# One broadcast load instead of four, VectorE work metered by time, and two small moves, in a kernel of two attention blocks

## The chip, the cores and the metric

One Trainium2 chip, one core. The time is the device time of one execution in microseconds (us). Most executions of a kernel agree within about half a percent here; every ratio below is between runs of the state "fast" made on the same chip in the same rounds; where ratios of different rounds are set side by side, the text says so. A run counts as slow when it is over 1.5% above the fastest of its kernel. Ratios of times are the mean time of one kernel's fast runs over the mean time of the other's fast runs of the same rounds, so they are not quite the ratio of the medians quoted beside them, which take in the slow runs too.

## The reference

Two independent attention blocks over 2048 tokens, width 448, 16 heads of 28 columns; their outputs stand side by side.

```python
# A: plain multi-head attention
p = softmax(q @ k.T * Dh ** -0.5);  a = (p @ v) @ wo
# B: four segments of 512 tokens; inside a segment causal attention,
#    and from the second segment on a memory of the segments before
a_dot = softmax(q @ k.T * Dh ** -0.5 + mask) @ v
num, den = phi(q) @ M, phi(q) @ z + 1e-06          # phi(t) = t+1 if t>0 else exp(t)
o = g * (num / den) + (1 - g) * a_dot              # g = sigmoid(beta), one per head
M = M + phi(k).T @ v;  z = z + sum(phi(k))
b = concat(o) @ wo
```

## The kernel before

The kernel is a static program of 375 slots. In each slot PE makes the scores of three banks (3 x 512 columns), ScalarE takes the exponential of all three in one instruction, and PE multiplies an earlier result by V. Everything else (projections, transposes, output products) is put between, a piece a slot. In PSUM the program holds six banks for scores, and a ring of two banks for all the rest, which VectorE evicts (copies out of PSUM, so that the bank is free again). VectorE also computes 60 banks of exponentials of its own in six instructions each: the eviction and five deferred ones.

Sixteen heads are handled four at a time; heads sit at partitions 0, 32, 64, 96. A finished accumulator holds the unnormalised output and, in row 28 of each head, the sum of the weights. To divide, the program turns the sums into reciprocals and spreads them over the 32 partitions of their head. That goes through DRAM in hops. "Planes" is 1 for A and for the first segment of B, 2 where a memory product is normalised as well:

```python
    def finish(key):                       # an accumulator is complete
        planes = 2 if side == "B" and s >= 1 else 1
        nc.vector.tensor_copy(out=o[:], in_=a[:])
        for n in range(planes):            # 4 rows of sums to DRAM
            nc.sync.dma_start(out=d1[n], in_=os_[n][DH:P:HP, :])
        def hop1():                        # 2 slots later: back, spread over 128 partitions
            nc.sync.dma_start(out=r[:, 0:planes, :], in_=d1...)
            later(3, step2)
        def step2():
            if planes == 2:
                nc.vector.tensor_scalar_add(r[:, 1, :], r[:, 1, :], 1e-6)
            nc.vector.reciprocal(r[:, 0:planes, :], r[:, 0:planes, :])
            ...                            # B: one multiply by a coefficient per plane
            nc.sync.dma_start(out=d2[0:planes]..., in_=r[:, 0:planes, :])
            at(state["u"] + 3, hop2)
        def hop2():                        # one row of 512 floats to 32 partitions, four times a plane
            for n in range(planes):
                bc = nrm.tile([P, CW], FP32, tag="nrm", name="bc")
                for j in range(4):
                    src = d2[n, j, :]
                    nc.sync.dma_start(out=bc[j * HP:(j + 1) * HP, :],
                        in_=bass.AP(tensor=src.tensor, offset=src.offset,
                                    ap=[[0, HP], [1, CW]]))
            later(4, *[lambda n=n: mul(n) for n in range(planes)])   # VectorE: o * bc
            if planes == 2:
                later(4, add)
```

`later(d, ...)` puts VectorE work into a queue, due d slots on. At the end of a slot's VectorE work this rule takes from it:

```python
    def run_bg(limit):                     # limit is 2
        for n in range(limit):
            ready = [x for x in bg if x[0] <= state["u"]]
            if not ready or n and len(ready) < 3 and limit < 8:
                return
            ...                            # run the oldest
```

The softmax here doesn't subtract the row's maximum and nothing guards it: scores larger than these inputs give would overflow.

## Time and profile before

| | before |
|---|---|
| median time, first 6 runs / all 20 runs beside the changed kernel | 559.06 / 559.37 us |
| span of the profiled run | 558.0 us |
| exponentials of ScalarE | 375, 1.33 us from start to start when nothing holds them |
| excess of ScalarE over 1.33 us each, sum | 30.2 us |
| of it at 0-40 / 40-160 / 160-200 / 200-380 / 380-end us | 5.2 / 2.4 / 1.7 / 10.8 / 10.1 us |

The excess is worked out from the trace: the start-to-start distance of neighbouring exponentials less 1.33 us, summed. Its parts leave out intervals with another ScalarE instruction between.

From the page of the kernel before: busy time of the engines, the granted PE clock in 40 slices of the span (tenths), the shares of the chain that ended last, and the costliest group (line, engine, operation, tiles, shapes, count | busy us, mean ns | idle before it, and who ended that).

```profile
PE 511.9 (92%) x5646; PEld 214.2 (38%) x5646; DVE 398.2 (71%) x919; ACT 526.2 (94%) x401; POOL 67.0 (12%) x136
PEclk9999999999999999999999999999999999978999
PE 39%; ACT 27%; DVE 19%; issue 10%; DMA 3%; SPq 2%; POOL 0%; DVEq 0%; ACTq 0%
L378 ACT ACTIVATE pt<-ps_s 128x1536 bf16<-128x1536 f32 x375 | 512.5, 1505 | 19.0 <-PE ps_s L373 17.5
```

ScalarE (ACT) is busy 94% of the span and bounds the kernel; its idle time ends when PE delivers scores. The clock dips once, in slices 36 and 37.

The waits list of the kernel before (engine, line, waited for: us in total, times, longest us), cut to ScalarE and to VectorE's waits for transfers:

```profile
ACT pt L378 <- PE ps_s L373: 17.5, 34, 1.9
...
DVE r L508 <- DMA r<-d_8398: 1.8, 1, 1.8
...
DVE oT L535 <- DMA bc<-d_6268: 1.0, 1, 1.0
```

VectorE (DVE) waited 1.0 us for a broadcast in the whole run. What the clock dip came from is read from three timelines of the kernel before (start us, us, what; in brackets the idle time before and who ended it). First SP, the queue that issues the loads:

```profile
488.10 1.03 SPq L495 DMA_DIRECT2D d_8398<-osb  x2
489.23 3.97 SPq L525 DMA_DIRECT2D bc<-d_8240  x8
493.24 0.42 SPq L500 DMA_DIRECT2D r<-d_8398  x1
```

Then VectorE:

```profile
493.17 0.39 DVE L596 CAST y<-ps_y 128x224 bf16<-128x224 f32 x1 [0.36 <-PE ps_y L590]
495.35 0.17 DVE L508 TENSOR_SCALAR r<-r 128x16 f32<-128x16 f32 x1 [1.79 <-DMA r<-d_8398]
495.56 0.35 DVE L509 RECIPROCAL r<-r 128x32 f32<-128x32 f32 x1
495.95 0.37 DVE L512 TENSOR_SCALAR r<-r,coef 128x16 f32<-128x16 f32 x2
496.23 0.38 DVE L596 CAST y<-ps_y 128x224 bf16<-128x224 f32 x1
```

Then PE:

```profile
494.53 0.40 PE L454 MATMUL acc<-pt,vA 128*32 128x512 bf16 x4
496.67 0.91 PE L590 MATMUL ps_y<-woA,oT 128*128 128x224 bf16 x4 [1.74 <-DVE y L596]
497.51 0.61 PE L373 MATMUL ps_s<-qTA,kTA 32*128 32x512 bf16 x3
```

Eight issues for one two-plane finish held SP for 4 us. The load of `r` stood behind them, VectorE stood before `r` for 1.79 us with an eviction behind it, PE idled 1.74 us for that eviction, and three score products then took 0.61 us instead of about 0.39: the trace records half the clock from 496.5 us for 10.24 us.

The other kind of stall is a queue in front of VectorE. VectorE at 357 us, kernel before:

```profile
357.23 0.69 DVE L489 COPY osb<-acc 128x512 f32<-128x512 f32 x1 [0.15 <-PE acc L454]
357.83 0.50 DVE L338 TENSOR_SCALAR vz<-vy 128x512 f16<-128x512 uint16 x1
358.37 0.43 DVE L343 TENSOR_TENSOR vq<-vz 128x512 f16<-128x512 f16 x1
358.83 0.29 DVE L344 TENSOR_SCALAR vz<-vz 128x512 f16<-128x512 f16 x1
359.04 0.69 DVE L476 COPY osb<-ps_mem 128x512 f32<-128x512 f32 x1
```

Two evictions (L489, L476) have deferred work between them; PE idled 1.02 us until the second, ScalarE 0.96 us.

### The profile page before, as it was taken

Reading aid. Unit: us, or ns where it says so; the run is one execution under the profiler, and the core shown is the slowest. Engines: PE = TensorE matmul, PEld = TensorE weight load, DVE = VectorE, ACT = ScalarE, POOL = GpSimd, SP = SyncE. Lnnn points to the kernel's source line nnn. Section 1 sums busy time; section 2 is a strip of 40 time slices with the busy share of each in tenths; the row PEclk is TensorE's granted clock in tenths of the full one; section 3 lists DMA queues with packets and bytes.
Section 4 is the critical chain, followed back from the end, with each engine's and each line's share of the span. In section 5 each row is a group of like instructions: output and inputs, shape, how many; then the busy total and the mean of one; then the engine's idle time right before and its main releaser. Section 6 shows DMA issues by size and latency. Waiting matters only on the chain.

```text
span 558.0 us, 13768 instructions
## 1 busy us (share of the span) xinstructions
PE 511.9 (92%) x5646; PEld 214.2 (38%) x5646; DVE 398.2 (71%) x919; ACT 526.2 (94%) x401; POOL 67.0 (12%) x136
## 2 busy tenths in 40 slices
PE   8899999999999998999989988889999998989996
PEld 4443443434443434334334333333344343323332
DVE  3438877776867587667687788875887886968742
ACT  5799999999999999999999999899999999978994
POOL 9100000000000000040040220210400401600000
PEclk9999999999999999999999999999999999978999
DMA  9100021000030110002002002012031031134121
GB/s 251 27 1 3 22 57 32 19 5 23 2 108 1 55 35 22 2 4 71 12 6 79 3 26 59 2 26 75 3 96 59 6 93 35 33 92 112 35 61 51
DMA packets 33623, 23.78 MB, mean 43 GB/s; under 512 B 16780, under 2 KB 27660, under 8 KB 33560
## 3 DMA queue, kind: packets, MB, share of 16 engines
q1 hardware_dynamic: 32216, 21.89, 14.0%
q0 software_dynamic: 416, 0.81, 0.7%
q8 instruction: 44, 0.72, 0.5%
q10 hardware_dynamic: 928, 0.21, 0.2%
q14 instruction: 19, 0.16, 0.1%
HBM read 18.51 MB, written 4.37 MB: 41 GB/s over the span
## 4 chain that ended last, share of the span: by engine, by line
PE 39%; ACT 27%; DVE 19%; issue 10%; DMA 3%; SPq 2%; POOL 0%; DVEq 0%; ACTq 0%
ACT pt L378 26%; PE ps_s L373 8%; PE acc L454 8%; PE ps_s L360 6%; PE ps_proj L209 5%; PE ps_v L223 5%; DVE osb L489 3%; SPq L525 2%; DVE vq L343 2%; DVE vy L334 1%; DVE vz L338 1%; DVE ve L351 1%; DVE vz L344 1%; PE ps_y L590 1%; DMA wstB<-in_B_wv_dram 1%
## 5 line engine op out<-in xcount | busy, mean ns | idle before, releaser
L378 ACT ACTIVATE pt<-ps_s 128x1536 bf16<-128x1536 f32 x375 | 512.5, 1505 | 19.0 <-PE ps_s L373 17.5
L373 PE MATMUL ps_s<-qTA,kTA 32*128 32x512 bf16 x964 | 129.3, 388 | 4.8 <-ACT pt L378 2.6
L454 PE MATMUL acc<-pt,vA 128*32 128x512 bf16 x964 | 124.3, 393 | 0.0
L360 PE MATMUL ps_s<-warm 128*128 128x512 bf16 x292 | 93.2, 382 | 11.8 <-ACT pt L378 10.1
L394 POOL TENSOR_SCALAR_AFFINE_SELECT pt<-pt 128x256 bf16<-128x256 bf16 (+5 forms) x110 | 52.1, 497 | 420.8 <-ACT pt L378 420.7
L373 PEld LDWEIGHTS <-kTA 32*128 32x128 bf16 x964 | 34.3, 91 | 94.2 <-issue 90.5
L454 PEld LDWEIGHTS <-vA 128*32 128x32 bf16 x1024 | 31.2, 93 | 71.6 <-issue 71.6
L209 PE MATMUL ps_proj<-xT,wstB 112*32 112x256 bf16 x1024 | 42.8, 274 | 7.8 <-DVE kTB L216 2.2
L209 PE MATMUL ps_proj<-xT,wstA 112*32 112x256 bf16 (+3 forms) x960 | 41.3, 281 | 1.5 <-DVE vy L334 0.5
L351 DVE SCALAR_TENSOR_TENSOR ve<-vy,vq 128x512 int16<-128x512 int32 x60 | 42.1, 702 | 0.3
L360 PEld LDWEIGHTS <-warm 128*128 128x128 bf16 x292 | 24.4, 97 | 39.8 <-issue 36.5
L223 PEld LDWEIGHTS <-xT 112*128 112x128 bf16 x352 | 28.2, 97 | 21.1 <-issue 19.0
L209 PEld LDWEIGHTS <-wstB 112*32 112x32 bf16 x1024 | 28.9, 96 | 18.4 <-issue 14.7
L209 PEld LDWEIGHTS <-wstA 112*32 112x32 bf16 x960 | 26.6, 95 | 14.2 <-issue 12.4
L596 DVE CAST y<-ps_y 128x224 bf16<-128x224 f32 x48 | 18.7, 389 | 18.0 <-PE ps_y L590 17.5
L489 DVE COPY osb<-acc 128x512 f32<-128x512 f32 x31 | 21.4, 690 | 9.4 <-PE acc L454 8.3
L343 DVE TENSOR_TENSOR vq<-vz 128x512 f16<-128x512 f16 x60 | 26.9, 448 | 1.6
L348 DVE TENSOR_TENSOR vq<-vq,vz 128x512 f16<-128x512 f16 x60 | 27.0, 451 | 0.2
L338 DVE TENSOR_SCALAR vz<-vy 128x512 f16<-128x512 uint16 x60 | 25.9, 431 | 1.1
L454 PE MATMUL acc<-ve,vA 128*32 128x512 bf16 x60 | 23.9, 399 | 0.0
L216 DVE TENSOR_SCALAR kTA<-ps_proj,live 128x256 bf16<-128x256 f32 (+3 forms) x29 | 14.8, 511 | 11.6 <-PE ps_proj L209 10.8
L454 PE MATMUL acc<-pt,vB 128*32 128x512 bf16 (+3 forms) x256 | 23.0, 306 | 0.0
(233 smaller groups left out, 491.7 us busy)
## 6 DMA issues: line engine op xcount, KB each, us to landing
out_dram<-y SPq DMA_DIRECT2D x32, 112.0 KB
xn<-in_A_x_dram SPq DMA_DIRECT2D x4, 448.0 KB
xnB<-in_B_x_dram SPq DMA_DIRECT2D x4, 448.0 KB
wstA<-in_A_wqkv_dram SPq DMA_DIRECT2D x2, 290.5 KB
bc<-d_4323 SPq DMA_DIRECT2D x8, 64.0 KB
bc<-d_4985 SPq DMA_DIRECT2D x8, 64.0 KB
bc<-d_5650 SPq DMA_DIRECT2D x8, 64.0 KB
bc<-d_6337 SPq DMA_DIRECT2D x8, 64.0 KB
```

The lines of the kernel that those rows point to most:

```text
L209: nc.tensor.matmul(ps[j * HP:(j + 1) * HP, a:b], lhsT=w[:, c, h0:h0 + HP], rhs=xT[:, c, sc * CW + a:sc * CW + b], start=(c == 0), stop=(c ...
L223: nc.tensor.matmul(ps, lhsT=xT[:, c, t * P:(t + 1) * P], rhs=w[:, c, c0:c0 + n], start=(c == 0), stop=(c == NKC - 1))
L338: nc.vector.tensor_scalar(out=z[:], in0=y[:].bitcast(U16).rearrange("p (c t) -> p c t", t=2)[:, :, 0], scalar1=2.0 ** -16, scalar2=Z0, op0 ...
L343: nc.vector.tensor_mul(q[:], z[:], z[:])
L348: nc.vector.tensor_mul(q[:], q[:], z[:])
L351: nc.vector.scalar_tensor_tensor(out=e[:].bitcast(I16), in0=y[:], scalar=2.0 ** -9, in1=q[:], op0=ALU.mult, op1=ALU.add)
L360: nc.tensor.matmul(ps[:, i % NB, :], lhsT=warm[:, 0:P], rhs=warm[:], start=True, stop=True)
L373: nc.tensor.matmul(ps[:, i, o0:o0 + w], lhsT=kk[rows, ko:ko + P], rhs=qq[rows, qo:qo + w], start=True, stop=True, tile_position=(j * HP, 0))
L378: nc.scalar.activation(out=pt[:, 0:n, :], in_=ps[:, 0:n, :], func=ACT.Exp, scale=scale)
L394: nc.gpsimd.affine_select(out=blk, in_=blk, compare_op=ALU.is_ge, fill=0.0, base=0, pattern=pat, channel_multiplier=-1)
L454: nc.tensor.matmul(acc[key][j * HP:(j + 1) * HP, a0:a0 + w], lhsT=v[:, t, h * HP:(h + 1) * HP], rhs=pt[:, i, c0:c0 + w] if i is not None e ...
L489: nc.vector.tensor_copy(out=o[:], in_=a[:])
```

## The change

Its intent: fewer issues on SP, VectorE work spread so that evictions come sooner, and a little less of that work. Five parts, cut to the core:

```diff
 # 1 one broadcast per plane
-                for j in range(4):
-                    src = d2[n, j, :]
-                    nc.sync.dma_start(
-                        out=bc[j * HP:(j + 1) * HP, :],
-                        in_=bass.AP(..., ap=[[0, HP], [1, CW]]))
+                src = d2[n, 0, :]
+                nc.sync.dma_start(
+                    out=bc[:],
+                    in_=bass.AP(..., ap=[[CW, 4], [0, HP], [1, CW]]))
 # 2 metering: each deferred item has a cost in us, each slot a budget
+BG = 0.8
+BGX = 0.4
-    def run_bg(limit): ...
+    def run_bg(room):
+        ready = sorted(x for x in bg if x[0] <= state["u"])
+        if sum(x[2] for x in ready) > 2.0:
+            room += BGX
+        for n, x in enumerate(ready):
+            if n and x[2] > room:
+                return
+            bg.remove(x)
+            x[3]()
+            room -= x[2]
-        later(1, fraction, square, cubic, whole)
+        later(1, (0.35, fraction), (0.55, square), (0.35, cubic), (0.6, whole))
-        run_bg(2 if u < nu else 8)
+        run_bg((BG - 0.4 * state["fin"]) if u < nu else 99)
     ...  (costs for the other items likewise)
 # 3 when a product with VectorE's own exponentials may join the others
-            if due > state["u"] or acc.get(key) is None:
+            if due > state["u"] or (key, b[4]) not in begun:
-            if b[4] in heads and left > mine + 8:
+            turns = [heads.count(j) for j in range(4)]
+            if (not heads or turns[b[4]] == max(turns)) and left > mine + 8:
 # 4 1e-6 in the copy of the memory product; both coefficients in one multiply
-        nc.vector.tensor_copy(out=o[:], in_=pm[:])
+        nc.vector.tensor_scalar_add(o[:], pm[:], eps[:])     # eps: 1e-6 in row 28 of each head
-                nc.vector.tensor_scalar_add(r[:, 1, :], r[:, 1, :], 1e-6)
 # 5 weights of B: V first
-        for i, src in enumerate((B_wq, B_wk, B_wv)):
+        for i, src in ((2, B_wv), (1, B_wk), (0, B_wq)):
```

More of the change, by code (lines that the diff above doesn't have):

```diff
@@ L132 @@
         axis=mybir.AxisListType.XY, op=ALU.add)
+    eps = const.tile([P, 1], FP32)
+    nc.vector.tensor_reduce(
+        out=eps[:], in_=ident[:].rearrange("p (j e) -> p j e", e=HP)[:, :, DH:DH + 1],
+        axis=mybir.AxisListType.XY, op=ALU.add)
+    nc.vector.tensor_scalar_mul(eps[:], eps[:], 1e-6)
     xnA.append(load_x(Ax, 1, "xn"))
@@ L277, in rows_of @@
                 in_=(omg, ecol)[i][:].rearrange("p (g j) -> p j g", j=4)[rows, j, :])
-        later(2, sig, *[lambda i=i, j=j: rows_of(i, j) for j in range(4) for i in range(2)])
+        later(2, (0.5, sig), *[(0.1, lambda i=i, j=j: rows_of(i, j))
+                              for j in range(4) for i in range(2)])
     banks = []
@@ L412 @@
     acc = {}
+    begun = set()
     acc_left = {}
@@ L426, with later @@
     bg = []
-    def later(d, *fns):
-        for n, fn in enumerate(fns):
+    def later(d, *items):
+        for c, fn in items:
             state["n"] += 1
-            bg.append((state["u"] + d, state["n"], fn))
-    def run_bg(limit):
-        for n in range(limit):
-            ready = [x for x in bg if x[0] <= state["u"]]
-            if not ready or n and len(ready) < 3 and limit < 8:
+            bg.append((state["u"] + d, state["n"], c, fn))
+    def run_bg(room):
[4 more added lines that the diff above has]
+            if n and x[2] > room:
                 return
-            x = min(ready)
             bg.remove(x)
-            x[2]()
+            x[3]()
+            room -= x[2]
     def at(u, fn):
@@ L458, in emit_pv_part @@
             start=first, stop=last, tile_position=(0, j * HP), skip_group_check=True)
+        begun.add((key, j))
         acc_left[key] -= 1
@@ L501, in hop1 @@
                               in_=d1[0:planes].rearrange("n j (i f) -> (j i) n f", f=16))
-            later(3, step2)
+            later(3, (0.15 + 0.3 * planes, step2))
         bcs = []
         def step2():
-            if planes == 2:
-                nc.vector.tensor_scalar_add(r[:, 1, :], r[:, 1, :], 1e-6)
             nc.vector.reciprocal(r[:, 0:planes, :], r[:, 0:planes, :])
             if side == "B":
-                for n in range(planes):
-                    nc.vector.tensor_scalar(out=r[:, n, :], in0=r[:, n, :],
-                                            scalar1=coef[:, n, g:g + 1], scalar2=None,
-                                            op0=ALU.mult)
+                c = coef[:, 0:planes, g:g + 1]
+                nc.vector.tensor_mul(r[:, 0:planes, :], r[:, 0:planes, :], bass.AP(
+                    tensor=c.tensor, offset=c.offset, ap=[c.ap[0], c.ap[1], [0, 16]]))
             nc.sync.dma_start(out=d2[0:planes].rearrange("n j (i f) -> (j i) n f", f=16),
@@ L522, in hop2 @@
                 bcs.append(bc)
-                for j in range(4):
-                    src = d2[n, j, :]
-                    nc.sync.dma_start(
-                        out=bc[j * HP:(j + 1) * HP, :],
-                        in_=bass.AP(tensor=src.tensor, offset=src.offset,
-                                    ap=[[0, HP], [1, CW]]))
-            later(4, *[lambda n=n: mul(n) for n in range(planes)])
+                src = d2[n, 0, :]
+                nc.sync.dma_start(
+                    out=bc[:],
+                    in_=bass.AP(tensor=src.tensor, offset=src.offset,
+                                ap=[[CW, 4], [0, HP], [1, CW]]))
+            later(4, *[(0.6, lambda n=n: mul(n)) for n in range(planes)])
             if planes == 2:
-                later(4, add)
+                later(4, (0.6, add))
         def mul(n):
@@ L698, in rest @@
             phiq[g, s] = ph
-        later(2, rest)
+        later(2, (0.8, rest))
     def knB(s, t, half):
@@ L722, in rest @@
                 done.add(("phik", s, t))
-            later(3, *[lambda t=t: rest(t) for t in range(4)])
+            later(3, *[(0.75, lambda t=t: rest(t)) for t in range(4)])
     def mB(s, gp):
@@ L746, in blocks @@
             nc.vector.tensor_copy(out=mblk[s][rows, gs, rows], in_=macc[rows, gs, :])
-        later(1, *[lambda j=j: blocks(j) for j in range(4)])
+        later(1, *[(0.15, lambda j=j: blocks(j)) for j in range(4)])
     table = {}
@@ L872, in run_pv @@
             n += 1
-        heads = {x[2][4] for x in batch}
+        heads = [x[2][4] for x in batch]
         for x in list(vready):
@@ L885, in run_pv @@
             state["ve"] -= 1
-            heads.add(b[4])
+            heads.append(b[4])
             taken[key] = taken.get(key, 0) + 1
```

## The prediction

> **What bounds the kernel now.** ScalarE. The page's head gives ACT 526.2 us busy of 558.0; the costliest group is 375 exponentials of 128x1536. From start to start two of them are 1.33 us apart when nothing is in the way (ScalarE's timeline), so no schedule of this program goes much below 375 x 1.33 + 12 = 511 us between first exponential (9.0) and last (549.2). That stretch is 540 us: about 29 us are excess. By time: 5 us before 40 us, 1.2 at 40 to 60, 1.1 where the V projection of B waits for its weights (168 us), about 11 scattered over 200 to 380 us, 7 at 490 to 513. Its waits name "PE ps_s" (17.5 us in 34), so what held PE matters.
>
> **What held PE, from PE's and VectorE's timelines.**
> - 200 to 380 us: PE waits for one of two ring buffers, which VectorE evicts late because deferred work stands ahead of it. At 357 to 360 us: osb 0.69, vz 0.43, vq 0.43, vz 0.29, osb of the memory product 0.69; PE idle 1.02 us, ScalarE 0.96.
> - 490 to 513 us: SP issues eight bc loads at 0.42 us each from 489.2 to 493.2, the r load stands behind them, VectorE waits 1.79 us for r, evicts y late, PE idles 1.74 us. The granted clock is then 0.5 for 10.24 us, which costs ScalarE about 5 us more. [...]
>
> **What the change does.**
> - Broadcast: 172 issues x 0.42 us on SP become 43. This should remove the stall at 494 us and the halved clock, about 5 us. But the source's outer dimension is 4: [...] so it may run on 4 engines, not 16. The trace agrees for the four-row stores (4 packets of 2048 B, 4 of 4 B; the 32-row loads show 16 of 4 B). Estimate: 32 packets x 0.084 us = 2.7 us a plane instead of 0.7, landing about 4 us after issue for one plane (3.5 now), 6.5 for the second (about 5 now). Mostly hidden.
> - Metering: at most about 0.8 us of deferred work a slot (1.2 with backlog, 0.4 less at a finish) instead of one or two items of any length. Evictions come sooner. I expect half of the 11 us.
> - 1e-6 in the copy: 12 x 0.17 us less; merged coefficient multiply about 2 us less VectorE work; nearly none of it critical.
> - V weights first: they land some 3 us earlier; about 1 us.
> - New stalls from shifted order: 1 to 2 us.
>
> Sum: 5 + 5.5 + 1 - 1.5 = about 10 us, less some because the halved clock may not occur in every timed run: **549.5 us** from 559.06. Range 543.5 to 557. Faster by over 2% 0.35, within 2% 0.61, slower 0.04.
>
> **Signs.** Right: clock 0.99 or more without a half-clock stretch before the tail; no idle PE over 1 us at 490 to 500; excess at 200 to 380 us down to about 6; no wait for wstB; SP bc issues 43. Wrong: VectorE waiting for bc in front of evictions, or a half-clock stretch elsewhere.
>
> **What would make it wrong.** A four-engine broadcast that lands late and stops VectorE at each finish; deferred work that piles up and ends later; another idle PE stretch that halves the clock again; the halved clock being rare in timed runs.

That the new load may run on 4 engines was my estimate, from the packets of 4 B of the four-row stores (4) and of the 32-row loads (16). That idle time of PE brings the halved clock rests here on the one stretch from 496.47 us, which began while PE was idle.

## The result, and the profile after

The changed kernel took **572.53 us** (median of 10 runs, 571.12 to 574.16) against 559.37 us of the kernel before (20 runs): ratio 1.024, 95% interval 1.0221 to 1.0259. It is slower by over 2%, and lies outside the predicted range of 543.5 to 557 us.

From the page after, the same lines:

```profile
PE 516.8 (91%) x5647; PEld 213.9 (37%) x5647; DVE 392.2 (69%) x897; ACT 526.3 (92%) x401; POOL 66.5 (12%) x136
PEclk9999999999999999999999999999996999987899
PE 35%; ACT 28%; DVE 15%; DMA 12%; issue 9%; SPq 1%; ACTq 0%; DVEq 0%
L387 ACT ACTIVATE pt<-ps_s 128x1536 bf16<-128x1536 f32 x375 | 512.7, 1489 | 31.4 <-PE ps_s L382 29.7
```

The work of ScalarE is the same (526.3 us), VectorE has 6 us less, and the span is 12.5 us longer. ScalarE's idle time before its exponentials rose from 19.0 to 31.4 us: that is the whole loss. On the chain that ended last, transfers went from 3% to 12%. There are three half-clock stretches before the tail (the last few us of the run) now, together 27.3 us (427.2, 509.1 and 522.8 us), in place of one of 10.2.

The waits list after, same cut (the six largest waits of VectorE for transfers):

```profile
ACT pt L387 <- PE ps_s L382: 29.7, 36, 3.4
...
DVE osb L544 <- DMA bc<-d_8127: 4.6, 2, 2.9
DVE osb L544 <- DMA bc<-d_6857: 4.5, 2, 2.9
DVE osb L544 <- DMA bc<-d_6275: 3.4, 2, 1.9
DVE oT L544 <- DMA bc<-d_6209: 3.2, 1, 3.2
...
DVE osb L544 <- DMA bc<-d_8281: 2.6, 2, 2.2
...
DVE osb L544 <- DMA bc<-d_6782: 1.3, 1, 1.3
```

Summed over the list, VectorE waits 26.6 us for `bc` in 19 places (26.9 with the smallest gaps, the number that the expectations below use), against 1.0 us in one. One such place, first on SP:

```profile
422.43 1.08 SPq L534 DMA_DIRECT2D bc<-d_6857  x2
```

On VectorE:

```profile
423.92 0.48 DVE L224 TENSOR_SCALAR kTB<-ps_proj,live 128x256 bf16<-128x256 f32 x1
427.33 0.69 DVE L544 TENSOR_TENSOR osb<-osb,bc 128x512 f32<-128x512 f32 x1 [2.92 <-DMA bc<-d_6857]
427.94 0.38 DVE L605 CAST y<-ps_y 128x224 bf16<-128x224 f32 x1
429.94 0.69 DVE L544 TENSOR_TENSOR osb<-osb,bc 128x512 f32<-128x512 f32 x1 [1.62 <-DMA bc<-d_6857]
430.55 0.38 DVE L605 CAST y<-ps_y 128x224 bf16<-128x224 f32 x1
```

And on PE:

```profile
425.26 0.40 PE L466 MATMUL acc<-pt,vA 128*32 128x512 bf16 x3
428.37 0.91 PE L599 MATMUL ps_y<-woB,oT 128*128 128x224 bf16 x4 [2.71 <-DVE y L605]
429.21 0.61 PE L382 MATMUL ps_s<-qTA,kTA 32*128 32x512 bf16 x3
```

SP is indeed done after 1.08 us. But the first plane lands 4.9 us after its issue, the second 7.5 us after it. VectorE stands in front of each, the eviction of `y` (L605) stands behind, PE idles 2.71 us, and the trace records half the clock for 10.24 us from 427.22 us, within that idle time. It is the same chain as at 494 us in the kernel before, with another transfer at its head.

How the loads ran is seen in the trace's records of DMA packets. They do not name the DMA engine; I take the packets of 4 B as one for each engine that takes part in a transfer, which is my reading. Counted for the first broadcast of each kernel, which has nothing beside it (a_twodma, a_row0 and a_rep16 are experiments below):

```
kernel     issues  packets of 2048 B  packets of 4 B   last 2048 B packet ends after the first issue
before        4          128            64 (16 each)      3.55 us
after         1          128             4                4.60 us
a_twodma      2          128             4 (2 each)       7.38 us
a_row0        1          128            16                2.77 us
a_rep16       1          128            16                2.73 us
```

How many packets of 2048 B ran at once agrees with that reading. In the first broadcast after, from its first such packet to the end of its last (3.24 us), 4 were in flight for 2.07 us and 5 or 6 for 0.43; in the first one before, up to 15. One took 0.084 us in both kernels (median). The source here is `[[CW, 4], [0, HP], [1, CW]]`, with 4 as its slowest dimension, and the load had 4 packets of 4 B. Slowest dimensions of 2 (a_twodma), 16 (a_rep16), 32 (the loads before) and 128 (a_row0) went with 2, 16, 16 and 16 of them a load. Other values were not tried.

The four busy engines have a second effect, which the chain of waits after shows for the same place (start us, us, what):

```profile
415.79 6.57 DMA d_6857<-r
...
423.00 6.91 DMA bc<-d_6857
```

The store of the reciprocals (`d_6857<-r`), issued 0.05 us after the two broadcasts of the finish before it, took 6.57 us. Its 256 packets of 64 B show why: 192 of them ran by 417.1 us, and the other 64, a quarter as four of 16 engines make it, only from 421.3 us, as the broadcasts' last packets ended (421.7 us). Twelve packets of 4 B were recorded by 417.04 us, and the last four from 421.84 us, after the broadcasts' eight. The load that needs this store then started late as well. From the issue of a store to the issue of its first load it is 3.86 us after (median of 31), 2.37 us before and 2.41 us in a_row0.

Where the excess lies by stretch, with some of the experiments beside it (us):

| stretch | before | after | b_onedma | a_fourdma | a_row0 | a_rep16 | r_strict | r_rush |
|---|---|---|---|---|---|---|---|---|
| 40-160 | 2.4 | 2.0 | 2.4 | 2.0 | 2.0 | 2.2 | 2.0 | 22.6 |
| 160-200 | 1.7 | 1.2 | 1.7 | 1.2 | 1.2 | 1.2 | 1.2 | 6.4 |
| 200-380 | 10.8 | 10.8 | 14.0 | 10.6 | 10.6 | 10.6 | 12.0 | 33.8 |
| 380-end | 10.1 | 23.8 | 18.8 | 10.9 | 5.1 | 5.7 | 5.2 | 49.5 |
| VectorE waits for bc | 1.0 | 26.6 | 18.5 | 8.7 | 4.5 | 4.8 | 3.9 | 5.2 |
| half clock before the tail | 10.2 | 27.3 | 20.5 | 6.8 | 0 | 0 | 6.8 | 92.2 |

The loss of the changed kernel lies after 380 us, where two-plane finishes crowd. The half clock differs from run to run (the mean granted clock of 28 timed runs of the kernel before lay between 0.984 and 1.0), so its row is of that one profile only, and it moves the rows above it as well: the 12.0 us of r_strict take in a half-clock stretch of 6.8 us at 284 us. The profile of b_onedma is of its fastest run.

### The profile page after: what moved, and what is told of

Its sections match the earlier page's. It is cut to its first block, busy times and chain, and to the rows that moved or that the text cites. A ratio compares the mean times of both kernels' runs of the same rounds, so it can differ in the third digit from the quotient of the medians.

```text
span 570.5 us, 13533 instructions
## 1 busy us (share of the span) xinstructions
PE 516.8 (91%) x5647; PEld 213.9 (37%) x5647; DVE 392.2 (69%) x897; ACT 526.3 (92%) x401; POOL 66.5 (12%) x136
## 4 chain that ended last, share of the span: by engine, by line
PE 35%; ACT 28%; DVE 15%; DMA 12%; issue 9%; SPq 1%; ACTq 0%; DVEq 0%
ACT pt L387 27%; PE ps_s L382 8%; PE acc L466 6%; PE ps_s L369 6%; PE ps_proj L217 5%; PE ps_v L231 3%; DVE osb L502 3%; DMA bc<-d_8281 2%; DMA bc<-d_6275 2%; DVE ve L360 1%; PE ps_y L599 1%; DMA d_8191<-r 1%; DMA bc<-d_6857 1%; DMA bc<-d_5603 1%; DMA d_6857<-r 1%
## 5 line engine op out<-in xcount | busy, mean ns | idle before, releaser
L387 ACT ACTIVATE pt<-ps_s 128x1536 bf16<-128x1536 f32 x375 | 512.7, 1489 | 31.4 <-PE ps_s L382 29.7
L466 PE MATMUL acc<-pt,vA 128*32 128x512 bf16 x964 | 125.7, 397 | 0.0
L231 PEld LDWEIGHTS <-xT 112*128 112x128 bf16 x352 | 28.1, 97 | 20.6 <-issue 19.4
L502 DVE COPY osb<-acc 128x512 f32<-128x512 f32 x31 | 21.4, 692 | 12.5 <-PE acc L466 11.4
L544 DVE TENSOR_TENSOR osb<-osb,bc 128x512 f32<-128x512 f32 x24 | 16.5, 689 | 19.6 <-DMA bc<-d_8127 4.6
L605 DVE CAST y<-ps_y 128x224 bf16<-128x224 f32 x48 | 18.7, 390 | 14.1 <-PE ps_y L599 13.4
L599 PE MATMUL ps_y<-woB,oT 128*128 128x224 bf16 x128 | 19.6, 280 | 7.6 <-DVE y L605 7.3
L352 DVE TENSOR_TENSOR vq<-vz 128x512 f16<-128x512 f16 x60 | 25.5, 424 | 0.2
L599 PEld LDWEIGHTS <-oT 128*128 128x128 bf16 x192 | 16.2, 102 | 23.6 <-issue 21.2
```

Of the source, the lines that this page charges most:

```text
L231: nc.tensor.matmul(ps, lhsT=xT[:, c, t * P:(t + 1) * P], rhs=w[:, c, c0:c0 + n], start=(c == 0), stop=(c == NKC - 1))
L387: nc.scalar.activation(out=pt[:, 0:n, :], in_=ps[:, 0:n, :], func=ACT.Exp, scale=scale)
L466: nc.tensor.matmul(acc[key][j * HP:(j + 1) * HP, a0:a0 + w], lhsT=v[:, t, h * HP:(h + 1) * HP], rhs=pt[:, i, c0:c0 + w] if i is not None e ...
L599: nc.tensor.matmul(ps[:, 0:n], lhsT=oT[side, s][:, g, t * P:(t + 1) * P], rhs=wo[:, g, half * n:(half + 1) * n], start=(g == 0), stop=(g = ...
```

## The experiments

Theory E: the one load runs on four engines and lands late; VectorE waits for it in order, with evictions behind. (The delay of the stores behind it: in a_mul5's expectation it is the second outcome.) Rival M: the metering and the new order bring the multiplies up earlier, and the load is harmless. Rival S: one large load with one semaphore lands late as such. Names with b_ are built on the kernel before, with a_ on the changed kernel.

### b_onedma: the kernel before with part 1 alone

```diff
-                for j in range(4): ...                 # four loads of 32 rows
+                nc.sync.dma_start(out=bc[:], in_=bass.AP(..., ap=[[CW, 4], [0, HP], [1, CW]]))
```

> The kernel before with one broadcast load per plane, nothing else. Theory E (few DMA engines): the load's source has 4 outer rows, so it runs on 4 engines (4 packets of 4 B each), lands 4.6 us after issue for one plane and about 7 us for the second instead of 3 and 5, and VectorE, which works in order, stands waiting for bc with evictions behind it. E expects most of the loss from this one part: 567 us or more, VectorE waits for bc of 12 us or more in all (1.0 in the kernel before), one or more half-clock stretches beyond the one of before. Rival M (metering and the new order put the multiplies earlier relative to the landing, the load itself is harmless): within 1% of the kernel before (553 to 565 us), VectorE waits for bc under 4 us.

580.09 us median (4 runs, 572.7 to 585.18, the last of them slow; before 558.88): ratio 1.0333, 1.026 to 1.0407. The waits list of its profiled run (a fast one):

```profile
ACT pt L378 <- PE ps_s L373: 27.5, 46, 5.0
DVE oT L534 <- DMA bc<-d: 11.0, 8, 2.6
DVE osb L534 <- DMA bc<-d: 7.5, 7, 1.7
```

18.5 us of waits for `bc` with no metering at all. The one part makes the whole loss (1.033 here, 1.024 in the changed kernel, in other rounds); rival M falls as the main cause.

### a_fourdma: the changed kernel with four loads per plane

```diff
-                nc.sync.dma_start(out=bc[:], in_=bass.AP(..., ap=[[CW, 4], [0, HP], [1, CW]]))
+                for j in range(4): ...                 # as in the kernel before
```

> The changed kernel with the four loads of 32 rows per plane put back, all other parts of the change kept. Theory E: VectorE waits for bc fall from 26.9 us to under 4 us, the half-clock stretches before the tail from three to one or none, time 548 to 559 us, thus no slower than the kernel before. Rival M: still 566 us or more. A third outcome, 560 to 565, would say that both carry part.

560.10 us median (4 runs; before 558.88): ratio 1.002, 0.9995 to 1.0046. The loss is gone, but so is any gain; the time lies at the edge of the third outcome. VectorE still waits 8.7 us for `bc` in 7 places, more than E allowed for. So M has a small part: with metering the multiplies do come up earlier relative to the landing (b_meter below shows 6.9 us of waits with the loads untouched).

### a_twodma: two loads of two source rows per plane

```diff
+                for j in (0, 2):
+                    src = d2[n, j, :]
+                    nc.sync.dma_start(out=bc[j * HP:(j + 2) * HP, :],
+                        in_=bass.AP(..., ap=[[CW, 2], [0, HP], [1, CW]]))
```

> The changed kernel with two loads of two source rows (64 partitions) per plane. If the engine count follows the source's outer dimension, each load runs on 2 engines, the same 2: 64 packets of 2048 B per engine and plane, about 5.5 us of transfer for one plane and 11 us for two, 4 packets of 4 B per plane. Theory E: slower than the changed kernel, 585 us or more, although it sits between one load and four in number and size. Rival S (what hurts is the size of one load or its single semaphore): between the four-load version and the changed kernel, under 572 us.

689.98 us median (4 runs; before 558.88): ratio 1.2341. In number and size it sits between the four-load version and the changed kernel, in time far outside both. Its clock slices and the two first waits of VectorE for transfers:

```profile
PEclk9999999999999998898699599599579689655688
```

```profile
DVE osb L545 <- DMA bc<-d: 75.7, 21, 5.5
DVE oT L545 <- DMA bc<-d: 31.1, 10, 5.5
```

Each load has two 4 B packets: two engines, by the reading above. Two planes took 12.6 us to land (median). The expectation of 585 us or more counted the waits too low: 106.8 us of them, and more than a dozen half-clock stretches.

### a_mul5: one load, multiplies due one slot later

```diff
-            later(4, *[(0.6, lambda n=n: mul(n)) for n in range(planes)])
+            later(5, *[(0.6, lambda n=n: mul(n)) for n in range(planes)])
```

> The changed kernel with its one broadcast per plane, but the multiplies by bc and the add come due 5 slots after the load's issue instead of 4, thus some 1.33 us later. Transfers are the same. Theory E with the wait in VectorE's order as the cause: VectorE waits for bc fall from 26.9 us to about 10 us, time 562 to 568 us. If instead the transfers hurt [...] (delaying the r loads and stores of d), the time stays at 571 us or more.

570.06 us median (5 runs, one of them slow; before 558.88): ratio 1.0188, 1.0154 to 1.0221. Less than E's waits alone would give back, more than the second outcome, in which nothing comes back. That fits both effects at work; their shares are not separated. Its profiled run was the slow one (12.9 us of waits for `bc` in it) and is not used, so the expected fall of the waits to about 10 us was not checked in a fast run. A version with 6 slots deadlocked in the simulation and was not run.

### b_meter, b_pv, b_smallv: the other parts alone

```diff
 # b_meter: part 2 alone;   b_pv: part 3 alone;   b_smallv: parts 4 and 5
```

> The kernel before with only the metering of deferred VectorE work by time. Prediction's step: ScalarE's excess between 200 and 380 us falls from 10.8 to about 6 us and the time to 553 to 556 us. Theory R (the direct evictions and the two ring buffers set those stalls, and the metering lifts its budget to 1.2 us just where work piles up): the excess stays within 1 us of 10.8 and the time within 0.5% of before.

561.09 us (4 runs; before 559.46): ratio 1.0026, 0.9976 to 1.0075. The excess at 200 to 380 us is 11.8 us, not 6; that profile has a half-clock stretch of 3.4 us at 340 us, so it does not show the metering doing harm, but it shows no gain.

> The kernel before with only the new rule for when a product with VectorE's own exponentials is put among the others. Nothing of the prediction rests on it; expected within 0.5% of before (556 to 562 us), with PE instructions in another order only.

559.96 us (4 runs): ratio 0.9998, 0.9975 to 1.0022.

> The kernel before with 1e-6 in the copy, one multiply for both coefficients and the V weights of B first. Prediction's step: the wait at 168 us (excess 0.85 us) goes, VectorE has some 3 to 4 us less to do; time 0.5 to 1.5 us less than before. If it is 2 us or more less, the small parts carry more than I gave them.

561.26 us (4 runs): ratio 1.0009, 0.9966 to 1.0052. The excess at 160 to 200 us fell from 1.7 to 1.1 us as expected, and nothing of it reaches the time: 0.6 us lies within the spread of the runs, and other stalls of that profile were larger (12.3 us at 200 to 380).

### a_four5, b_mul5, a_split5: the time of the multiplies, and SP's queue

```diff
 # a_four5: a_fourdma with later(5, ...) for the multiplies and the add
 # b_mul5:  the kernel before with later(5, ...) for them
 # a_split5: a_four5, and the second plane's loads one slot after the first's
```

> The changed kernel with four loads per plane and the multiplies due 5 slots after the issue instead of 4. In the four-load version VectorE still waited 8.7 us for bc in 7 places. If those waits are what keeps that version from being faster than before, they fall under 3 us and the time to 553 to 557 us; if they were harmless, it stays at 558 to 561 us.

556.65 us (4 runs; before 559.46): ratio 0.9944, 0.9916 to 0.9972. Waits for `bc` fell to 2.8 us.

> The kernel before with its multiplies due 5 slots after the issue, nothing else. The kernel before waits only 1.0 us for bc, so nothing is to be won: within 0.4% of before (557 to 561 us). If it reaches a_four5's 0.994, the metering had no part in that gain.

560.50 us (4 runs; before 560.69): ratio 0.9999, 0.9961 to 1.0038. Nothing, as expected. So the later multiply helps only together with the rest of the change (0.9944 in a_four5, in other rounds).

> The four-load version with multiplies 5 slots after issue, and the second plane's loads issued one slot after the first's, so that other loads of SP can go between. The half-clock stretch at 500 us came from an r load behind eight bc issues. If that queue still costs, 553 to 556 us and no r wait; if not, as a_four5 (555 to 558 us).

557.97 us (4 runs; before 560.69): ratio 0.995, 0.9913 to 0.9987. The same as a_four5: no more to be had from splitting the queue. One idle time of PE of 1.9 us and one half-clock stretch of 6.8 us remained, at 514 to 523 us.

### a_row0: one load, 16 engines, wrong result on purpose

```diff
-                                ap=[[CW, 4], [0, HP], [1, CW]]))
+                                ap=[[0, P], [1, CW]]))          # every partition reads row 0
```

> Wrong result on purpose: the changed kernel, still one load of 256 KB per plane, but each of the 128 partitions reads row 0, so the source has one outer dimension of 128 instead of 4 and 32. Bytes, packets, issues and every other instruction are the same. Theory E: 16 packets of 4 B per load instead of 4, last packet about 3.2 us after issue for one plane and under 4.5 us for two, VectorE waits for bc under 3 us, no half-clock stretch from them: 551 to 558 us. Rival S (one large load with one semaphore lands late as such): 568 us or more.

553.61 us (4 runs; before 560.69): ratio 0.9875, 0.9843 to 0.9907. This is the sharpest test: one access pattern differs, with the same bytes, packets and issues. (The comparison with the reference passed; presumably the four heads' reciprocals are near enough for its tolerance, which was not looked into. The result is wrong by construction all the same.) Clock slices and waits of VectorE for transfers:

```profile
PEclk9999999999999999999999999999999999999999
```

```profile
DVE oT L544 <- DMA bc<-d: 2.5, 1, 2.5
DVE osb L544 <- DMA bc<-d: 2.0, 2, 1.2
```

The load has 16 packets of 4 B and lands as early as the four loads of the kernel before (medians over all finishes 2.95 us for one plane and 4.57 for two, against 2.98 and 4.88). The clock is never halved before the tail. The waits, 4.5 us, are above the 3 us expected, the time is inside its range. Rival S falls: with 16 packets of 4 B, one load of 256 KB with one semaphore made no loss (0.9875). Against the changed kernel's 1.024, which is from other rounds, the number of engines is worth some 3.6% (1.024 / 0.9875).

### a_rep16: the same with a right result

The reciprocals are stored four times each, in rows that follow one another, so that the load's slowest dimension is 16.

```diff
-        d2 = dram.tile([2, 4, CW], ...)
+        d2 = dram.tile([2, 4, 4, CW], ...)
+                nc.sync.dma_start(                     # per plane; partition = 4 * i + j
+                    out=bass.AP(d2[n], ap=[[16, HP], [4 * CW, 4], [CW, 4], [1, 16]]),
+                    in_=bass.AP(r[:, n, :], ap=[r.ap[0], [0, 4], [1, 16]]))
-                                ap=[[CW, 4], [0, HP], [1, CW]]))
+                                ap=[[CW, 16], [0, 8], [1, CW]]))
 # r is loaded in the order (i, j), and the coefficients are turned into it once
```

> Right result: the changed kernel with the reciprocals stored four times in DRAM, so that one load per plane reads 16 source rows of which each serves 8 partitions, and runs on 16 engines. It adds 512 packets of 64 B per plane to the store and one more small load and store issue for a second plane. Theory E: as a_row0 but for a store that lands later: VectorE waits for bc under 6 us, 552 to 559 us. It beats the kernel before by over 0.5% only if the later store stays hidden.

556.20 us (4 runs; before 560.69): ratio 0.9925, 0.9886 to 0.9964. It is right and beats both kernels, by 0.75% (the interval is clear of 1, though not by 2%) and, by the two ratios from different rounds, some 3%. It is 2.6 us behind a_row0 (556.20 less 553.61); the larger store (512 packets of 64 B a plane in place of 128, so 384 more and not 512 as the expectation says) and the additional small issues were not tried apart.

### r_rush, r_strict, r_mul5: the metering again, on the base a_rep16

```diff
-BG = 0.8
+BG = 99.0        # r_rush: everything that is due runs at once
+BG = 0.6         # r_strict
 # r_mul5: multiplies due 5 slots after the issue
```

> The version with replicated rows (one load on 16 engines) with the budget per slot set so high that every deferred item that is due runs at once. If deferred items ahead of evictions set the stalls of 200 to 380 us, the excess there grows from 10.6 us to 14 us or more and the time by 3 us or more (559 us or more). If direct evictions and the ring set them, the excess stays within 1.5 us of 10.6 and the time within 0.5% of the base (553 to 559 us).

651.79 us (4 runs; before 559.58): ratio 1.1623. Waits of ScalarE in its profile:

```profile
ACT pt L398 <- PE ps_s L393: 99.8, 112, 3.9
```

> The same version with the budget per slot at 0.6 us instead of 0.8. If the metering was only too loose, the excess of 200 to 380 us falls to 8 us or less and the time to 554 us or less. If deferred items do not set those stalls, the excess stays within 1.5 us of 10.6.

556.29 us (4 runs; before 559.58): ratio 0.9936, 0.9879 to 0.9994, beside 0.9925 of its base in other rounds. The excess at 200 to 380 us is 12.0 us.

> The same version with the multiplies due 5 slots after the issue. VectorE's waits for bc fall from 4.8 us to under 2 us; time 552 to 556 us if those waits still cost, unchanged if they do not.

555.37 us (4 runs; before 559.58): ratio 0.993, 0.9872 to 0.9988: the same as its base, so the last waits for `bc` (2.7 us here) cost nothing that is seen.

Deferred work ahead of evictions does set stalls, and large ones: without any limit the excess at 200 to 380 us is 33.8 us, with what the half clock adds. But the old rule of one or two items a slot already had that gain. A budget in microseconds adds nothing to it in that stretch, and a tighter one adds nothing either. What sets the 10.6 us that are left was not shown; the timeline at 357 us suggests the two direct evictions of a finish in one slot with two ring buffers, which no run here removed.

## Why the prediction was wrong, point by point

- **"What bounds the kernel now" was right.** ScalarE's work is the same before and after, and the time follows its excess.
- **The four-engine estimate was nearly right, its consequence was not.** The prediction said that the load "may run on 4 engines" and would land "about 4 us after issue for one plane (3.5 now), 6.5 for the second (about 5 now)". The last packets ended 4.3 and 7.1 us after issue (medians), against 3.0 and 4.9 before. The step that failed is the next one: "**Mostly hidden.**" VectorE's waits for `bc` went from 1.0 to 26.6 us. The trace of before showed that there was no room: in six of its 19 one-plane finishes the multiply began within about 1 us of the last packet (0.43 to 1.01 us), and in one of these it had waited. I read how long a load takes, and not how long after the load its reader comes. Four slots are 5.3 us, but they run from the slot and not from the issue: SP works in order too, and in the tight cases the load stood behind a store of the next finish (at one of them the accumulator was copied at 290.24 us, its store issued at 290.96 and the load at 292.09).
- **What I had not thought of at all is that other transfers queue behind the broadcast,** such as the store of 6.57 us above. This matters most for the finishes with two planes, on which 19.4 of the 26.6 us of waits fall. In the kernel before they mostly had room for the later landing alone: in eleven of the twelve the second multiply began 2.2 to 5.4 us after the last packet (0.49 us in the other), and the landing became 2.2 us longer. But the load is now also issued later, 3.86 us after its store instead of 2.37, and its multiplies stay due at the same slots. The prediction counted from the issue and left this out. How much of those 19.4 us the late issue makes, and how much the metering with its earlier multiplies, was not taken apart; with the load alone (b_onedma) finishes with two planes waited 7.5 us and those with one 11.0 us.
- **"This should remove the stall at 494 us and the halved clock, about 5 us" failed in the changed kernel** for the same cause: the SP queue was freed as said (1.08 us for two planes instead of 3.7, medians), and a wait for `bc` took the place of the wait for `r`. Three half-clock stretches came for one. With 16 engines (a_row0, a_rep16) the step holds: no half clock before the tail, excess after 380 us 5.1 and 5.7 us instead of 10.1.
- **"I expect half of the 11 us" from metering failed on its own.** b_meter has ratio 1.0026 and 11.8 us of excess there, and the changed kernel has 10.8 us as before. The old rule by count had already limited deferred work; r_rush shows what that limit is worth, r_strict that more of it is worth nothing.
- **"about 1 us" for the V weights first** was nearly right in the trace (0.6 us) and too small to be seen in the time.
- **"nearly none of it critical" for the smaller VectorE work** was right: b_smallv is at 1.0009.
- **Of the dangers named,** "deferred work that piles up" was not seen, and "the halved clock being rare" came in part: 14 of the 28 timed runs of the kernel before that were made beside the experiments had a mean granted clock above 0.991, the figure of the profiled run with its 10.24 us of half clock. The three at 0.998 or more took 557.0 to 557.8 us against a median of 559.6 of all 28, so that the half clock looks worth some 2 to 2.5 us of the median (an estimate from few runs); the prediction's 5 us counted the stall at 494 us with it. "A four-engine broadcast that lands late and stops VectorE at each finish" was named too, and with the stores that it holds up it was nearly the whole: a_fourdma, without it, is at 1.002. Its chance was put far too low: 0.04 for slower.
- The traces show what makes a short wait dear. Each of the four half-clock stretches before the tail, one before and three after, began while PE was idle: 1.54 us into an idle time in the kernel before (from 494.93 us, by the modelled end of its last matmul, to 496.47); in the changed kernel 1.56 us into one (425.66 to 427.22), 0.38 us (508.76 to 509.14, where PE had also idled 2.54 us from 504.67) and 2.57 us (520.22 to 522.79). None began in that 2.54 us, or in the other idle times of PE, the longest of them 1.32 us. The stretches told of here lasted 3.4 (b_meter), 6.8 or 10.2 us. At 427 us PE idled 2.71 us, and the excess of ScalarE between 420 and 440 us was 6.2 us.

What stays open: how the waits divide between the late landing, the late issue and the earlier multiplies; which of the other parts gives a_rep16 its 0.75% together with the good load, since the good load was not tried on the kernel before; and what sets the remaining excess at 200 to 380 us.

## What to carry to other kernels

When several transfers become one, compare first the slowest dimension of the source and the count of 4 B packets in the trace, before and after. Here a plane of 256 KB took 4.60 us as one load with 4 of them, 2.77 us as one with 16, and 7.38 us as two loads with 2 each, from the first issue to the end of the last packet. Before calling a longer transfer hidden, measure in the trace the time from the transfer's end to its reader, on the tightest occurrence and not on the mean; here VectorE, working in order, passed a wait of 2.92 us for `bc` on to the eviction behind it, and PE idled 2.71 us for that eviction. And before a finer limit on deferred work is given a gain, find out what the coarse one already has, for instance by lifting it.
